# Attention with V read in 8 KB rows: quads of heads and 64x64 tiles for PV

## The chip, the core and the metric

One core of a Trainium2 chip runs the kernel. The metric is the device time of one execution in microseconds (us). The kernel before takes 340.26 us (median of 3 runs, 340.18 to 340.37).

The engines are TensorE (PE, with its weight loads shown apart as PEld), VectorE (DVE), ScalarE (ACT), GpSimd (POOL) and SyncE (SP), which issues the DMA transfers. TensorE reads its operands from SBUF and writes PSUM.

## The reference

```python
B, Hq, Hkv, Sq, Sk, D = 16, 32, 8, 16, 2048, 128     # bfloat16, inputs scaled by 0.05
k = jnp.repeat(k, 4, axis=1)
v = jnp.repeat(v, 4, axis=1)
scores = jnp.einsum("bhqd,bhkd->bhqk", q, k) * D ** -0.5
p = softmax(scores)
return jnp.einsum("bhqk,bhkd->bhqd", p, v)
```

Four query heads share one K/V head, so each of the 128 K/V heads meets 4 x 16 = 64 query rows. K and V are 67.1 MB each, Q and the output 2.1 MB each.

## The kernel before

The unit of work is a pair of K/V heads: 64 units, with 128 query rows (64 per head) by 2,048 keys each.

SP issues all transfers on one queue, in the order of the loop over `t` (L198): K of unit `t` (`load_k`, 1 MB, 128 rows of 8 KB, four buffers `Kn`), Q of four units at a time (`load_q`), the first half of a store, V of a unit further back (`load_v`, 1 MB), the second half of the store. V is read as two rows of 4 KB per partition, one per head; it has eight buffers `Vb`, and `v_lag` puts it two to five units behind K. K waits until the unit four before has been transposed, V until PV of the unit eight before is done, a store until its output is normalised. V of the last unit comes in three pieces (`CUTS`).

Per unit `i`, each engine runs its own list and meets the others at semaphores:

- DVE (`emit`, L350): reads the scores from PSUM, scales and negates them into `Sneg` and takes the row minimum (L353); takes the reciprocal of the row sum before (L361); transposes K of unit `i + 2` in 32x32 blocks, in two instructions (`kt`, L344).
- PE (loop from L282): `scores` of unit `i + 1` (32 matmuls in tiles of 32 rows by 64 columns, 512 columns each: four tiles at a time, one for each row group; every second group of four, L219, uses the weights that L248 loaded); `pv` of unit `i - 3` (L266: 32 matmuls of 128 rows by 64 columns, two column groups); eight transposes of the probabilities (`turn_p`, L257); in two of four units four transposes of Q (`turn_q`, L231), which have a PSUM bank of their own.
- ACT: `exp` into `P` (L391); the norm of unit `i - 3` out of `O_ps` (L409); the copies of the transposed probabilities (`p_out`, L399) and of the transposed Q (`q_out`, L380).
- POOL: spreads Q for the transposes (L152).

PE's loop covers eight units, as do DVE's and ACT's. The scores have one PSUM buffer, so `scores` of a unit waits for L353 of the unit before. The last three units' outputs go to banks of `S_ps`.

## Time and profile before

| | |
|---|---|
| median of 3 runs | 340.26 us |
| profiled execution, own time | 340.08 us |
| its span, first to last instruction | 338.3 us |
| TensorE clock granted, mean | 0.995 |
| bytes moved, mean rate | 138.55 MB, 410 GB/s |
| busy: PE, DVE, ACT, POOL | 278.0, 295.4, 267.8, 31.3 us |
| K, V transfers: issue to landing (median) | 14.9, 15.5 us |

The profile is one execution. Its slices are 40 equal parts of the span, with the busy share in tenths. The DMA row is the mean share of the core's 16 DMA engines. The chain of work is followed back from the last instruction; "SPq" in it is SP's queue of DMA issues. A group's line gives the line of the code, engine, operation and tiles, then busy time, mean ns of one instruction, and the engine's idle time before these instructions with what ended it. Matmuls overlap, so their mean duration is longer than the distance between them.

### The profile page before, as it was taken

What the parts mean: (1) busy time and instruction counts of PE and PEld (TensorE: products, weight loads), DVE (VectorE), ACT (ScalarE), POOL (GpSimd) and SP (SyncE); (2) the same over time, 40 slices, a digit from 0 to 9 for tenths busy, and PEclk for the clock granted to TensorE, in tenths of its full rate; (3) what the DMA queues carried; (4) which work ended last, traced back from release to release, by engine and by line L of the source; (5) the groups of instructions that cost most, each with busy time, mean ns of one, the idle gap of its engine ahead of it and who ended that gap; (6) DMA issues with size and microseconds to landing.
All of it is one profiled execution on the core that took longest, in us unless ns stands there. A gap on an engine that the chain in (4) does not pass through costs nothing.

```text
span 338.3 us, 9752 instructions
## 1 busy us (share of the span) xinstructions
PE 278.0 (82%) x4736; PEld 159.2 (47%) x3712; DVE 295.4 (87%) x321; ACT 267.8 (79%) x355; POOL 31.3 (9%) x22
## 2 busy tenths in 40 slices
PE   0687999979898798979898797787888878888885
PEld 0133555535554454545355454454454454453454
DVE  2499999989998999989999988989889889899860
ACT  1178888888989788978888787877977878778785
POOL 3202020201102020200202010020200202000000
PEclk9979999999999999999999999999999999999999
DMA  7999999999999999999999999999999999999996
GB/s 299 417 417 412 412 412 413 420 416 422 416 417 417 424 414 419 419 417 421 418 421 414 422 418 415 419 419 418 421 417 418 421 414 418 421 418 422 416 413 213
DMA packets 39642, 138.55 MB, mean 410 GB/s; under 512 B 12496, under 2 KB 15056, under 8 KB 31440
## 3 DMA queue, kind: packets, MB, share of 16 engines
q1 hardware_dynamic: 39632, 138.43, 100.7%
q8 instruction: 5, 0.08, 0.1%
q14 instruction: 5, 0.04, 0.0%
HBM read 136.31 MB, written 2.10 MB: 409 GB/s over the span
## 4 chain that ended last, share of the span: by engine, by line
SPq 65%; DMA 18%; DVE 6%; PE 4%; issue 3%; ACT 2%; POOL 1%; ACTq 0%
SPq L195 37%; SPq L163 13%; SPq L171 11%; DMA Kn<-in_k_dram 9%; DMA Vb<-in_v_dram 8%; SPq L184 4%; DVE KT L344 3%; DVE Sneg L353 3%; ACT P L391 2%; DMA Qn<-in_q_dram 1%; PE ST_ps L257 1%; PE S_ps L248 1%; PE ST_ps L231 1%; PE S_ps L219 1%; POOL Q L152 1%
## 5 line engine op out<-in xcount | busy, mean ns | idle before, releaser
L344 DVE STREAM_TRANSPOSE KT<-Kn 128x1024 f32<-128x1024 f32 x128 | 151.5, 1222 | 27.6 <-DMA Kn<-in_k_dram 27.6
L391 ACT ACTIVATE P<-Sneg,nbias 128x2048 bf16<-128x2048 f32 (+1 forms) x65 | 160.1, 2463 | 8.8 <-DVE Sneg L353 8.8
L353 DVE TENSOR_SCALAR_CACHE_REDUCE Sneg<-S_ps 128x2048 f32<-128x2048 f32 x64 | 144.3, 2255 | 6.3 <-PE S_ps L219 6.3
L248 PE MATMUL S_ps<-KT,QT 32*64 32x512 bf16 x1024 | 102.8, 393 | 16.8 <-DVE Sneg L353 15.8
L219 PE MATMUL S_ps<-KT,QT 32*64 32x512 bf16 x1024 | 101.2, 387 | 0.0
L266 PEld LDWEIGHTS O_ps<-Vb,PT 128*64 128x64 bf16 x1952 | 57.2, 110 | 66.4 <-issue 66.4
L266 PE MATMUL O_ps<-Vb,PT 128*64 128x128 bf16 x1952 | 66.2, 220 | 25.7 <-DMA Vb<-in_v_dram 25.7
L399 ACT ACTIVATE PT<-ST_ps 128x512 f32<-128x512 f32 x128 | 69.7, 595 | 19.0 <-PE ST_ps L257 18.4
L257 PE MATMUL ST_ps<-ident,P 128*128 128x128 f32 x512 | 71.0, 282 | 5.9 <-ACT P L391 5.7
L248 PEld LDWEIGHTS S_ps<-KT,QT 32*64 32x64 bf16 x1024 | 28.9, 104 | 84.2 <-issue 47.6
L257 PEld LDWEIGHTS ST_ps<-ident,P 128*128 128x128 f32 x512 | 55.4, 142 | 15.4 <-ACT P L391 11.1
L152 POOL COPY Q<-Qn 128x2048 bf16<-128x2048 bf16 x16 | 30.3, 1893 | 254.2 <-DMA Qn<-in_q_dram 185.2
L409 ACT ACTIVATE O<-O_ps,rrec 128x128 bf16<-128x128 f32 x61 | 22.4, 368 | 30.2 <-PE O_ps L266 29.9
L231 PE MATMUL ST_ps<-ident,Q 128*128 128x128 f32 x128 | 20.4, 284 | 8.6 <-POOL Q L152 7.9
L380 ACT ACTIVATE QT<-ST_ps 128x512 f32<-128x512 f32 x32 | 19.3, 605 | 8.3 <-PE ST_ps L231 8.3
L231 PEld LDWEIGHTS ST_ps<-ident,Q 128*128 128x128 f32 x128 | 15.7, 147 | 9.0 <-issue 7.9
L391 ACT ACTIVATION_READ_ACCUMULATOR P<-Sneg,nbias 128x1 f32 x65 | 13.3, 205 | 0.0
L361 DVE RECIPROCAL rrec<-rowsum 128x1 f32<-128x1 f32 x63 | 9.9, 157 | 0.0
L353 DVE DVE_READ_ACCUMULATOR Sneg<-S_ps 128x1 f32 x64 | 5.3, 82 | 0.0
L266 PE MATMUL S_ps<-Vb,PT 128*64 128x128 bf16 x96 | 3.6, 221 | 0.8 <-DMA Vb<-in_v_dram 0.7
L266 PEld LDWEIGHTS S_ps<-Vb,PT 128*64 128x64 bf16 x96 | 2.9, 110 | 1.6 <-DMA Vb<-in_v_dram 1.1
L372 DVE TENSOR_TENSOR rowsum<-rowsum 128x1 f32<-128x1 f32 x1 | 0.2, 160 | 3.4 <-ACT P L391 3.4
(9 smaller groups left out, 3.7 us busy)
## 6 DMA issues: line engine op xcount, KB each, us to landing
Kn<-in_k_dram SPq DMA_DIRECT2D x64, 1024.0 KB, 14.9
Vb<-in_v_dram SPq DMA_DIRECT2D x63, 1024.0 KB, 15.5
Qn<-in_q_dram SPq DMA_DIRECT2D x16, 128.0 KB, 14.7
out_dram<-O SPq DMA_DIRECT2D x118, 16.0 KB, 14.2
Vb<-in_v_dram SPq DMA_DIRECT2D x1, 512.0 KB, 9.6
Vb<-in_v_dram SPq DMA_DIRECT2D x1, 320.0 KB, 9.8
Vb<-in_v_dram SPq DMA_DIRECT2D x1, 192.0 KB, 9.8
out_dram<-O SPq DMA_DIRECT2D x5, 32.0 KB, 1.9
```

The costliest lines, as they stand in the source:

```text
L163: sp.dma_start(Kn[s][:, :], kf[p]).then_inc(sem_k[p % BODY], 16)
L171: sp.dma_start(dst, vf[:, 2 * p:2 * p + 2, :]).then_inc(sem_v[s], 16)
L195: sp.dma_start(of[128 * p + 64 * x:128 * p + 64 * x + n, :], Osb[s][64 * x:64 * x + n, :]).then_inc(sem_o[s], 16)
L219: return pe.add_instruction(mybir.InstMatmult(name=nc.get_next_instruction_name(), engine=mybir.EngineType.PE, ins=[pe.lower_ap(rhs), pe.l ...
L231: ins = pe.transpose(dst[:, 128 * j:128 * (j + 1)], src[:, j, b, :], ident4[:, :])
L248: ins = pe.matmul(s_ap, w, x, start=(acc == 0), stop=(acc == 3))
L257: ins = pe.transpose(dst[:, 128 * t:128 * (t + 1)], P[p % 2][:, 128 * x:128 * (x + 1)], ident4[:, :])
L266: ins = pe.matmul(o_ap(at)[64 * g:64 * (g + 1), :], pt[:, j // 2, j % 2, 64 * g:64 * (g + 1)], Vb[p % NV][:, g, j, :], start=(j == 0), sto ...
L344: ins = dve.transpose(KT[p % NKT][:, :].rearrange("p (t b e a x) -> p x e t b a", t=J // 2, b=2, e=2, x=2)[:, x, :, :, :, :], Kn[p % NK][: ...
L353: dve.tensor_scalar(Sneg[i % 2][:, :].rearrange("p (t h x) -> p h t x", t=8, h=2), S_ps[:, :].rearrange("p (h t x) -> p h t x", t=8, h=2), ...
L391: act.activation(P[i % 2][:, :].bitcast(BF16)[:, cols].rearrange("p (n y e) -> p n y e", y=64, e=2), Sneg[i % 2][:, cols].rearrange("p (n ...
L399: ins = act.activation(PT[i % NPT][:, 4 * h:4 * (h + 1), :].rearrange("p t q -> p (t q)"), stage_ap(h), ACT.Copy,)
```

## The change

Two units now make a quad of four neighbouring K/V heads `4d` to `4d + 3`.

- K: unit `u = 2d + i` holds heads `4d + i` and `4d + 2 + i`. Partition `2a + g` gets 8 KB of head `4d + 2g + i`, so a transfer reads 128 rows of 8 KB from two places 1 MB apart. There are eight K buffers in one tensor `Kd`.
- V: a transfer is two neighbouring heads, 128 rows of 8 KB, one per partition: 64 partitions per head, 32 groups of 64 keys. There are two buffers `Vd` of a quad (2 MB) each, so V of a quad waits for PV of two quads before (`sem_pv`). V of the last two quads goes into K's buffers 0 to 3. The last two transfers are one of 2 MB in four pieces (rows of 4 KB, 2 KB, 1.25 KB and 0.75 KB).
- The lag of V behind K is 2 and 6 units for the first four, then 11, less one every eight units, down to 7. Stores of the first 28 quads stay in the loop; the last four are issued behind all loads, the very last half by ACT.
- Scores: 32 matmuls in eight tiles (four row groups by two column groups) in turn, each with its own weight load.
- `P` holds a quad, with its two units interleaved, so `turn_p` of a unit needs `exp` of both and comes two units later (`TLAG`). PV is 64 matmuls per unit, 64 rows by 64 columns: two row groups (heads `i`) by two column groups (`g`), in two banks of `O_ps`. It comes six units after the unit's `exp`, half a quad per step.
- `turn_q` is eight transposes of 64 rows for each two units; its output shares the first bank of `ST_ps` with `turn_p`, so `turn_p` of even steps waits for ACT's copy of Q, and `turn_q` waits for ACT's copies of the probabilities (`sem_po`).
- PE's loop covers four units, with the last two quads under an `If` in the same loop. A step of PE is, in this order: scores of the next unit, on even steps `turn_q`, half a quad of PV, on even steps the wait for ACT's copy of Q, `turn_p`. An even step of ACT is `exp`, the copy of Q, two copies of `turn_p`; an odd one `exp`, two copies, two norms.
- DVE transposes K in one instruction per unit instead of two. It takes over the norms of the last four quads, with ACT doing half of the last one.

```diff
-NK = 4
-NV = 8
-NKT = 2
+NK = 8
+NV = 2
+NP = 2
 NPT = 4
-NO = 8
-NQ = 2
+NO = 4
+NQ = 4
 QPAIRS = 4
-BODY = 8
-VLAG = 5
-PVLAG = 3
-SLAG = 10
-QLEAD = 4
-CUTS = (0, 8, 13, 16)
+ROUND = 8
+STEP = 4
+VLAG = 7
+PVLAG = 6
+TLAG = 2
+SLAG = 6
+QLEAD = 6
+CUTS = (0, 16, 24, 29, 32)
...
-    Kn = [sb(f"Kn{i}", [128, 2 * J * 128], BF16) for i in range(NK)]
-    Vb = [sb(f"Vb{i}", [128, 2, J, 128], BF16) for i in range(NV)]
-    KT = [sb(f"KT{i}", [128, 2 * J * 64], F32) for i in range(NKT)]
+    ident = sb("ident", [128, 128], F32)
+    Kd = sb("Kd", [128, NK, 32 * D], BF16)
+    Vd = [sb(f"Vd{i}", [128, 2, J, D], BF16) for i in range(NV)]
+    KT = [sb(f"KT{i}", [128, J * 64], F32) for i in range(2)]
...
-    P = [sb(f"P{i}", [128, Sk // 2], F32) for i in range(2)]
-    PT = [sb(f"PT{i}", [128, J // 2, 128], F32) for i in range(NPT)]
+    P = [sb(f"P{i}", [128, J // 2 * 128], F32) for i in range(NP)]
+    PT = [sb(f"PT{i}", [128, J // 4, 128], F32) for i in range(NPT)]
...
-    ST_ps = ctx.enter_context(nc.psum_tensor("ST_ps", [128, 3 * 512], F32))
-    O_ps = ctx.enter_context(nc.psum_tensor("O_ps", [128, 512], F32))
+    ST_ps = ctx.enter_context(nc.psum_tensor("ST_ps", [128, 2 * 512], F32))
+    O_ps = ctx.enter_context(nc.psum_tensor("O_ps", [128, 2 * 512], F32))
...
-    of = out.rearrange("b h s d -> (b h s) d")
-    kf = k.rearrange("b h s d -> (b h s d)").rearrange("(n a x) -> n a x", n=NP, a=128)
-    vf = v.rearrange("b h s d -> (b h) (s d)").rearrange("g (a x) -> a g x", a=128)
+    of = out.rearrange("b h s d -> (b h s) d").rearrange("(n g i x) d -> n i g x d", n=ND, g=2, i=2)
+    kf = k.rearrange("b h s d -> (b h s d)").rearrange("(n g i a x) -> n i a g x", n=ND, g=2, i=2, a=64)
+    vf = v.rearrange("b h s d -> (b h s d)").rearrange("(n a x) -> n a x", n=NU, a=128)
...
     def v_lag(p):
-        return min(2 + max(p - 4, 0) // 8, VLAG)
+        return 2 if p < 2 else 6 if p < 4 else max(VLAG, 11 - (p - 4) // 8)
+
...
+    def q_ap():
+        return ST_ps[:, 0:512].rearrange("p (b x) -> p b x", b=2)
+
+    def o_ap(d, i):
+        x = 512 * i
+        if d >= ND - 2:
+            return S_ps[:, 1024 * (d % 2) + x:1024 * (d % 2) + x + D]
+        return O_ps[:, x:x + D]
+
+    def v_ap(d, g):
+        if d >= ND - 2:
+            return Kd[:, 2 * (d % 2) + g, :].rearrange("p (j d) -> p j d", j=J)
+        return Vd[d % NV][:, g, :, :]
...
+    def store_both(eng, d, g):
+        dst = of[d, :, g].rearrange("i x d -> x i d")
+        eng.dma_start(dst, Osb[d % NO][64 * g:64 * (g + 1), :, :]).then_inc(sem_o[d % NO], 16)
...
-            def load_k(p):
-                s = p % NK
-                if p >= NK:
-                    sp.wait_ge(sem_kt[(p - NK) % BODY], (p - NK) // BODY + 1)
-                sp.dma_start(Kn[s][:, :], kf[p]).then_inc(sem_k[p % BODY], 16)
+            def load_k(m):
+                s = m % NK
+                if m >= NK:
+                    sp.wait_ge(sem_kt[s], m // NK)
+                sp.add_instruction(mybir.InstDMACopy(
+                    name=nc.get_next_instruction_name(), engine=mybir.EngineType.SP,
+                    ins=sp.lower_ap_dma(kf[m // 2, m % 2]), outs=sp.lower_ap_dma(Kd[:, s, :].unsqueeze(1)),
+                    queue="qSPDynamicHW", mode="Copy", cce_op=ALU.bypass,
+                )).then_inc(sem_k[s], 16)
 
             def load_v(p):
...
+                d, g = divmod(p, 2)
+                if p >= NU - 2:
+                    if g:
+                        return
+                    sp.wait_ge(sem_kt[3], ROUNDS)
+                    for x, (lo, hi) in enumerate(zip(CUTS, CUTS[1:])):
+                        src = vf[p:p + 2, :, D * lo:D * hi].rearrange("g a x -> a g x")
+                        sp.dma_start(Kd[:, 2:4, D * lo:D * hi], src).then_inc(sem_vl[1 + x], 16)
                     return
...
+                if d == ND - 2:
+                    sp.wait_ge(sem_kt[g], ROUNDS)
+                elif d >= NV and g == 0:
+                    sp.wait_ge(sem_pv[d % NV], d // NV)
+                sp.dma_start(v_ap(d, g).rearrange("a j d -> a (j d)"), vf[p]).then_inc(
+                    sem_v[d % NV] if d < ND - 2 else sem_vl[0], 16)
...
+            def turn_q(x):
+                rows = slice(64 * x, 64 * (x + 1))
                 src = Q4[:, :, :, :, :].bitcast(F32).rearrange("p j b r c -> p j b (r c)")
...
+                for b in range(2):
+                    for j in range(QPAIRS):
+                        ins = pe.transpose(q_ap()[:, b, 64 * j:64 * (j + 1)], src[rows, j, b, :], ident[rows, rows])
+                ins.then_inc(sem_qt[x], 1)
+
+            def scores(u):
+                d, i = divmod(u, 2)
+                kt = KT[i][:, :].bitcast(BF16).rearrange("p (b y g e) -> p b e g y", b=2, g=2, e=2)
+                qt = QT[d % 2][:, :, :].bitcast(BF16).rearrange("p b (n e) -> p b e n", e=2)
                 for acc in range(4):
                     b, e = divmod(acc, 2)
...
+                    for z in range(8):
+                        r, g = z % 4, (z + z // 4) % 2
+                        rows = slice(32 * r, 32 * (r + 1))
+                        at = 128 * g + 64 * i
                         ins = pe.matmul(
...
+                            S_ps[64 * g:64 * (g + 1), 512 * r:512 * (r + 1)],
+                            qt[rows, b, e, at:at + 64], kt[rows, b, e, g],
+                            start=(acc == 0), stop=(acc == 3),
                         )
...
+                ins.then_inc(sem_s[u % STEP], 1)
...
+                        y = 8 * (w % 2) + 4 * h + t
+                        ins = pe.transpose(ST_ps[:, 512 * h + 128 * t:512 * h + 128 * (t + 1)],
+                                           P[w // 2 % NP][:, 128 * y:128 * (y + 1)], ident[:, :])
+                    ins.then_inc(sem_pt[h][w % STEP], 1)
...
+            def pv(d, js, gs=(0, 1)):
+                for j in js:
+                    pt = PT[(2 * d + j // 16) % NPT][:, :, :].bitcast(BF16).rearrange("p t (q e) -> p t e q", e=2)
+                    for g in gs:
+                        for i in range(2):
+                            rows = slice(64 * i, 64 * (i + 1))
+                            ins = pe.matmul(
+                                o_ap(d, i)[64 * g:64 * (g + 1), :],
+                                pt[rows, j % 16 // 2, j % 2, 64 * g:64 * (g + 1)],
+                                v_ap(d, g)[rows, j, :],
+                                start=(j == 0), stop=(j == J - 1),
+                                skip_group_check=True,
+                            )
+                return ins
...
+                def step_s(i):
+                    pe.wait_ge(sem_max[i], now)
+                    scores(i + 1)
+
+                def step_q(i):
+                    x = i // 2
+                    if x == 0:
+                        pe.wait_ge(sem_q4, then)
+                    pe.wait_ge(sem_po[(i - TLAG - 1) % STEP], now)
+                    turn_q(x)
+
+                def step_pv(i):
+                    d, half = divmod((i - PVLAG) % STEP, 2)
+                    if half == 0:
+                        pe.wait_ge(sem_v[d], v_now)
+                        pe.wait_ge(sem_nm[1 - d], it)
+                        pe.nop(nofuse=True)
+                    ins = pv(d, range(16 * half, 16 * half + 16))
+                    if half:
+                        ins.then_inc(sem_pv[d], 1)
+
+                def step_pt(i):
+                    w = (i - TLAG) % STEP
+                    if w == 0:
+                        pe.wait_ge(sem_exp[1], now)
+                    pe.wait_ge(sem_po[(w - 1) % STEP], it if w == STEP - 1 else now)
+                    turn_p(w)
+
+                with pe.If(it >= TURNS + 1):
+                    pe.wait_ge(sem_po[1], TURNS + 1)
+                    turn_p(NU - 2)
+                    pe.wait_ge(sem_po[2], TURNS)
+                    turn_p(NU - 1)
+                    pe.wait_ge(sem_vl[0], 32)
+                    pe.nop(nofuse=True)
+                    pv(ND - 2, range(J)).then_inc(sem_pe, 1)
+                    for x, (lo, hi) in enumerate(zip(CUTS, CUTS[1:])):
+                        if lo == 16:
+                            pe.wait_ge(sem_po[3], TURNS + 1)
+                        pe.wait_ge(sem_vl[1 + x], 16)
+                        pe.nop(nofuse=True)
+                        ins = pv(ND - 1, range(lo, hi))
+                    ins.then_inc(sem_pe, 1)
...
+            def kt(u, n):
+                dve.wait_ge(sem_k[u % NK], n)
+                dve.transpose(
+                    KT[u % 2][:, :].rearrange("p (b j a) -> p j b a", b=2, j=J),
+                    Kd[:, u % NK, :].bitcast(F32).rearrange("p (j b c) -> p j b c", b=2, c=32),
+                ).then_inc(sem_kt[u % NK], 1)
...
+                    exp(i, None, sem_exp[i % STEP])
+                    if i % 2 == 0 and not (at.end and i >= 4):
+                        y = (i + 4) // 2
+                        q_out(y % 2, at.num(2, y // 2 + 1))
+                    if at.first or i >= TLAG:
+                        p_out(i - TLAG, at.tile(i - TLAG))
+                    if i % 2 and (at.first or i >= PVLAG + 1):
+                        y = (i - PVLAG - 1) // 2
+                        act.wait_ge(sem_pv[y % NV], at.num(2, y // NV + 1))
+                        if at.first >= 2 or (at.first == 1 and y >= 0):
+                            act.wait_ge(sem_o[y % NO], at.num(64, 64 * (y // NO)))
+                        for z in range(2):
+                            x = (2 * y + z) % ROUND
+                            ins = act.activation(Osb[y % NO][:, z, :], o_ap(y % NO, z), ACT.Copy, scale=rrec[:, x:x + 1])
+                        ins.then_inc(sem_nm[y % NV], 1)
...
```

## The prediction

> **What bounds the kernel now.** I read the page's slices and DMA parts first, then the chain, then a table by stretch, and only then the engines' groups.
>
> ```profile
> DMA  7999999999999999999999999999999999999996
> ...
> DMA packets 39642, 138.55 MB, mean 410 GB/s; under 512 B 12496, under 2 KB 15056, under 8 KB 31440
> ...
> q1 hardware_dynamic: 39632, 138.43, 100.7%
> ...
> SPq 65%; DMA 18%; DVE 6%; PE 4%; issue 3%; ACT 2%; POOL 1%; ACTq 0%
> ```
>
> The DMA engines are full from the second slice to the last but one, and the chain runs mostly through SP's DMA issues (SPq) and the transfers themselves. No compute engine carries more than 6% of it. By stretch (length; PE, PEld, DVE, ACT, POOL busy; clock, DMA share, GB/s):
>
> ```profile
> 0.00:10.00 10.00, 1.36 (x6) 0.99 (x7) 3.38 (x3) 1.88 (x2) 2.85 (x7) 1.00 0.80 319
> ...
> 100.00:200.00 100.00, 85.81 (x1493) 49.47 (x1168) 93.69 (x102) 84.27 (x113) 9.47 (x5) 1.00 1.03 418
> 200.00:300.00 100.00, 82.11 (x1423) 47.94 (x1117) 89.22 (x99) 80.07 (x108) 9.47 (x5) 1.00 1.03 419
> ...
> 330.00:338.00 8.00, 4.81 (x104) 3.70 (x104) 0.33 (x2) 4.58 (x10) 0.00 (x0) 1.00 0.62 216
> ```
>
> A share of 1.03 says that one engine's packets overlap a little and that no gap is left. 10 us at 319 GB/s is 7.6 us of work at 419, so the start loses 2.4 us; the last V piece lands at 335.5 (waits of the last PV) and norm and store take the remaining 2.8. Compute follows the stream, but not by far:
>
> ```profile
> L344 DVE STREAM_TRANSPOSE KT<-Kn 128x1024 f32<-128x1024 f32 x128 | 151.5, 1222 | 27.6 <-DMA Kn<-in_k_dram 27.6
> L391 ACT ACTIVATE P<-Sneg,nbias 128x2048 bf16<-128x2048 f32 (+1 forms) x65 | 160.1, 2463 | 8.8 <-DVE Sneg L353 8.8
> L353 DVE TENSOR_SCALAR_CACHE_REDUCE Sneg<-S_ps 128x2048 f32<-128x2048 f32 x64 | 144.3, 2255 | 6.3 <-PE S_ps L219 6.3
> ...
> L266 PE MATMUL O_ps<-Vb,PT 128*64 128x128 bf16 x1952 | 66.2, 220 | 25.7 <-DMA Vb<-in_v_dram 25.7
> ```
>
> DVE's and PE's longest waits are for DMA. Where nothing waits, Sneg starts come 4.53 us apart (38.43, 42.96, 47.50), with 5.3 per unit over the run. The rates of single pieces, from the timeline:
>
> ```profile
> 308.24 1.09 PE L257 MATMUL ST_ps<-ident,P 128*128 128x128 f32 x8
> ...
> 308.93 1.08 ACT L399 ACTIVATE PT<-ST_ps 128x512 f32<-128x512 f32 x2 [0.22 <-PE ST_ps L257]
> ...
> 309.26 0.42 PE L248 MATMUL S_ps<-KT,QT 32*64 32x512 bf16 x4
> ...
> 309.51 0.39 PE L219 MATMUL S_ps<-KT,QT 32*64 32x512 bf16 x4
> ...
> 309.74 0.39 PE L248 MATMUL S_ps<-KT,QT 32*64 32x512 bf16 x4
> ...
> 312.28 1.09 PE L266 MATMUL O_ps<-Vb,PT 128*64 128x128 bf16 x32 [1.03 <-DMA Vb<-in_v_dram]
> ```
>
> Four score matmuls of 0.39 us, one per row group, fill 0.39 to 0.42: they start within 0.03, and the next four 0.225 us later. Sixteen PV pairs take (1.09 - 0.22)/15 = 58 ns a pair, so two column tiles run side by side.
>
> **The change, step by step.** Base: the profiled execution, 340.08 us (span 338.3 and 1.8 around it); the median is 0.18 more.
>
> *V rows.* The trace's packet records (size, start, duration) give means of 311.0 ns for 8,192 B (K) and 160.0 ns for 4,096 B (V). On one engine the next packet starts 3.2 and 3.7 ns before the end, so the pitches are 307.8 and 156.4 ns. (39,632 packets over 16 engines with 3.5 ns each are 2.6% of the span: the 1.03.) 62 of the 64 V transfers become 128 rows of 8 KB: 496 rows per engine, each in place of two. 496 x (312.8 - 307.8) = 2.5 us less. Ends: 0, if bytes and not packets set the stream's rate; 4.5, if whole durations count (496 x 9.1 ns). I take 2.5, since the pitch is what adds up to the span. The last 2 MB keep rows of 4 KB and less, and stores (256 B rows) and Q loads move the same rows on the same queue: 0.
>
> *K from two places.* Rows stay 8 KB, but neighbouring partitions now come from heads 1 MB apart. Nearest row: V before, two heads 512 KB apart, ran at the 160 ns above. So 0; ends: no gain is open, as rows were 8 KB; if they cost as two 4 KB rows, 512 x 5.0 ns = 2.6 us more.
>
> *SP's order and its new wait.* SP issues K, stores, V; V of a quad waits for PV of two quads earlier, and Q, K and stores stand behind it. Ahead of the first such wait are 16 K, 4 V, 6 Q: 21.8 MB, at 419 GB/s 51.9 us, done at 54.3 with the start. PV of quad 0 ends in step 7: Sneg 6 starts at 43.0, +2.3, exp 2.7 and some 0.6 of ACT lag (four steps of 4.7 against 4.53, below) gives 48.5, Q copy 0.6, eight P transposes 1.1, scores 1.0, PV half 0.9: 52.2. The first bytes move 1.7 us after the first issue (0.7 to 2.4): 53.9, before 54.3. So 0, with 0.4 to spare; ends 0 and 2 us (slow tiles, next). Later the stream holds five transfers (12.5 us) between a quad's last V and the next waiting V, PV takes a step and a half-step (6.2): 4.6 to spare, and the store's wait for the norm stands one wait behind, on work already done. POOL's Q copy (1.9) waits for the second Q transposes and has two steps, 9.4, until the next: 0.
>
> *Scores.* Eight tiles in turn instead of four, with a weight load each (32, were 16): four rounds of 0.225 = 0.9 us, was 1.8; ends 0.9 and 1.8. *PV.* 64 matmuls per unit with 64 rows; row groups overlap in the scores and column groups in PV, so four at once: 16 x 58 ns = 0.93 us; ends 0.93 and 1.86. No row has both kinds at once. Both lie beside DVE and ACT; what counts is the chain.
>
> *The shared staging bank.* Q transposes now use P's first bank, so on even steps: exp 2.58 (with its accumulator read, as rows stand), Q copy 0.6, then P transposes may start, 0.05 + 0.69 to the first copy (308.24 to 308.93), copies 1.08: 5.0. Odd steps: 2.58 + 1.08 + two norms 0.7 = 4.4. ACT needs 9.4 per two units, 4.7 each. DVE has one transpose in place of two (2.3 to 2.4) and stays at 4.5. The stream asks for less: K 0 lands near 5, the last K eight V before the end (333 - 20 = 313), 308/63 = 4.88 per unit. ACT's 4.7 hides under that with 0.18 a unit; if that cover goes, each 0.1 costs up to 6 us over 61 steps, less what the early K and the V waits absorb (some 5 us).
>
> *The end.* After the last K: transpose 2.4, Sneg 2.3 twice, exp in halves 3, both units' copies, done 16 us on; PV of quad 30 1.9, of 31 mostly before its last piece: 19 against the stream's 20. So the last piece ends it as now: 12 matmuls, norm, store, 2.8. Ends 0 and 2.7 (PV at half rate: two quads and the last pieces). DVE's and ACT's norms and ACT's own store run side by side: 0.
>
> Sum: 340.08 - 2.5 = 337.6, median **337.8 us**; own range 336.0 to 339.6.
>
> **Rivals.**
>
> *A. PV doesn't run at four tiles (slower).* At 29 ns per matmul (58/2) PV takes 1.86 per unit. In the odd step PE ends the even step's P transposes 4.35 after exp's start, then scores 1.05, PV 1.86 and 0.69 to the first copy: 7.95, later than exp's end at 7.6; with copies 1.08 and norms 0.7 the cycle is 9.75 (4.88 a unit, all cover gone), about 1 us of stream is lost near the first V wait, and the end is 2.7 late: 337.8 + 3.7 = 341.5. Taken as linear from 14.5 ns (0) to 29 (3.7), it eats the 2.5 from 24 ns per matmul on. For it: PV's own row shows nothing faster. Against: four score matmuls start within 30 ns. [...]
>
> *B. Neither tile form overlaps.* Scores stay 1.8 too: 4.35 + 1.95 + 1.86 + 0.69 + 1.78 = 10.6, 5.3 a unit: (5.3 - 4.88) x 61 = 26 us, 363. Against it: both overlaps stand in the rows, apart.
>
> *C. K's new layout slows its packets* (engines meeting at the same partitions). K's packets are 512 x 308 ns = 158 us per engine; 5% more is 8 us, 346. No row for or against the destination side.
>
> *D. Bytes set the rate:* 340.2, no change; the even 411 to 424 GB/s of the slices speak for it, the packet records against.
>
> *E. Whole durations count:* 340.26 - 4.5 = 335.8.
>
> **Chances.** Forecast 0.60, A 0.13, B 0.05, C 0.06, D 0.09, E 0.07. Within 0.2% (0.7 us) is no change here: D and a slice of A, 0.10; slower: the rest of A, B, C, 0.22; faster 0.68. Range 335.4 to 342.5: it takes in E and A and leaves B and most of C out.
>
> **What would show it.** Fewer packets (about 31,700), DMA share still 1.02 in the middle at some 422 GB/s, chain on SPq again; eight score matmuls in one group of 0.4; PV spans near 0.93 per 64 matmuls; ACT waiting for PE after Q copies by 0.7. Wrong would be: slices with DMA below 9 near 54 us or later, K packets longer than 311 ns, PE or ACT leading the chain, a tail over 3 us after the last V piece.

## The result and the profile after

The changed kernel takes 353.02 us (median of 4 runs, 352.80 to 353.29) beside 340.31 us of the kernel before on the same chip: a ratio of 1.037, 95% interval 1.036 to 1.039. It is slower by 12.7 us; 2.5 us less were forecast. The profiled execution took 353.29 us with a span of 351.5.

The page of the changed kernel, its slices, its DMA parts and the first line of the chain:

```profile
PEclk9956869999999999999999999999999989999998
...
DMA  7999993699999999999999999999999999999993
GB/s 275 426 415 419 414 402 137 267 397 419 423 418 394 418 422 425 418 420 424 421 423 420 422 426 420 421 421 422 423 419 422 421 421 423 424 424 419 329 407 110
...
DMA packets 31659, 138.57 MB, mean 394 GB/s; under 512 B 12448, under 2 KB 15008, under 8 KB 15520
...
q8 instruction: 6, 0.10, 0.1%
...
PE 42%; ACT 28%; DMA 10%; issue 10%; DVE 4%; SPq 4%; POOL 1%; ACTq 0%
```

Three things differ from before. There are about 8,000 packets fewer, as meant. The DMA row has a hole in the seventh and eighth slices, and the GB/s row a dip in the last three. The chain no longer runs through SP's issues but through PE, ACT and "issue", time in which an engine waited for nothing that the profile shows. The clock granted to TensorE (PEclk) is low in the third to the sixth slice. By stretch (length; PE, PEld, DVE, ACT, POOL busy; clock, DMA share, GB/s):

```profile
56.00:60.00 4.00, 3.86 (x104) 2.50 (x88) 4.00 (x5) 2.73 (x4) 1.89 (x1) 1.00 0.02 8
60.00:64.00 4.00, 4.00 (x106) 2.23 (x104) 3.85 (x2) 3.59 (x5) 0.00 (x0) 1.00 0.00 0
100.00:200.00 100.00, 90.26 (x2264) 52.51 (x2256) 93.75 (x85) 84.43 (x116) 9.46 (x5) 1.00 1.02 418
200.00:300.00 100.00, 89.77 (x2185) 51.81 (x2169) 92.35 (x81) 82.58 (x112) 9.46 (x5) 0.98 1.02 422
```

From 56.5 to 63 us next to nothing moves. From 200 to 300 us the stream runs at 422 GB/s, which was 419 before; from 100 to 200 us, in which SP stands 4.2 us at a further V wait (to 111.4), it is 418 both before and after. SP's issues around the hole, from the timeline of the changed kernel:

```profile
51.42 0.54 SPq L187 DMA_DIRECT2D Kd<-in_k_dram  x1
63.13 0.33 SPq L207 DMA_DIRECT2D Vd<-in_v_dram  x1
```

SP stands for 11.2 us at the wait of `load_v` for PV of quad 0, whose second half PE does at 61.99 to 63.08. PE is late because its own list stood still in its first turn (the timeline again; idle time before an instruction in brackets):

```profile
19.47 1.56 PE L269 MATMUL S_ps<-KT,QT 32*64 32x512 bf16 x23 [5.30 <-issue]
...
24.97 1.08 PE L269 MATMUL S_ps<-KT,QT 32*64 32x512 bf16 x9 [3.94 <-issue]
...
38.44 1.77 PE L280 MATMUL ST_ps<-ident,P 128*128 128x128 f32 x8 [2.89 <-issue]
```

The scores of one unit stop after 23 of 32 matmuls, with every operand there. (Of the 5.30 us before their first part, 2.4 are the wait for DVE, whose `Sneg` of unit 0 ends at 16.5.) Beside these stops the trace has the six 16 KB packets of the row "q8 instruction": at 16.7, 22.5, 29.1, 35.3, 41.2 and 46.8 us, and none later. Each takes 1.0 to 1.1 us, and the three starts above come 1.5 to 2.1 us after the end of such a packet. Before, there were four in the same stretch, at 21.9, 30.9, 41.6 and 49.3 (and a fifth at 333.5); the page before has

```profile
q8 instruction: 5, 0.08, 0.1%
```

The low clock stands beside the stops: 0.50 was granted from 20 to 26 us and 0.52 from 26 to 32, and the eight P transposes of 1.09 us take 1.77 at 38.44, where 0.56 was granted.

To see where the time is, I counted for each stretch what the stream lost against 421.5 GB/s (length less the bytes of the kernel's own transfers over that rate), up to the landing of the last V, and the rest of the span as the end:

| us | 0 to 10 | 10 to 48 | 48 to 80 | 80 to 305 | 305 to last load | end | span |
|---|---|---|---|---|---|---|---|
| before | 2.6 | 0.8 | 0.4 | 1.6 | 1.4 | 3.3 | 338.3 |
| after | 3.1 | 0.5 | 10.1 | 0.7 | 2.7 | 6.2 | 351.5 |
| difference | +0.6 | -0.2 | +9.7 | -0.9 | +1.2 | +3.0 | +13.2 |

So the questions were: why PV of quad 0 is late (9.7 us), and what the end is made of (3.0 us).

### The profile page after: what moved, and what is told of

The parts are those of the page before. It is cut to its first block, busy times and chain, and to the rows that moved or that the text cites. A ratio compares the mean times of both kernels' runs of the same rounds, so it can differ in the third digit from the quotient of the medians.

```text
span 351.5 us, 15443 instructions
## 1 busy us (share of the span) xinstructions
PE 284.7 (81%) x6912; PEld 166.0 (47%) x6912; DVE 293.5 (83%) x264; ACT 260.8 (74%) x348; POOL 31.3 (9%) x22
## 4 chain that ended last, share of the span: by engine, by line
PE 42%; ACT 28%; DMA 10%; issue 10%; DVE 4%; SPq 4%; POOL 1%; ACTq 0%
PE S_ps L269 19%; ACT P L454 15%; PE ST_ps L280 13%; PE O_ps L290 9%; DMA Vd<-in_v_dram 7%; ACT PT L463 5%; DVE Sneg L403 4%; ACT QT L445 4%; ACT O L493 3%; DMA Kd<-in_v_dram 2%; SPq L222 2%; DMA Qn<-in_q_dram 1%; PE ST_ps L256 1%; SPq L207 1%; DVE KT L395 1%
## 5 line engine op out<-in xcount | busy, mean ns | idle before, releaser
L395 DVE STREAM_TRANSPOSE KT<-Kd 128x2048 f32<-128x2048 f32 x64 | 147.0, 2297 | 12.9 <-DMA Kd<-in_k_dram 12.7
L269 PE MATMUL S_ps<-KT,QT 32*64 32x512 bf16 x2048 | 128.4, 624 | 26.8 <-DVE Sneg L403 16.8
L280 PE MATMUL ST_ps<-ident,P 128*128 128x128 f32 x512 | 71.9, 285 | 20.1 <-ACT QT L445 13.2
L290 PEld LDWEIGHTS O_ps<-Vd,PT 64*64 64x64 bf16 x3840 | 56.3, 108 | 33.3 <-issue 31.7
L280 PEld LDWEIGHTS ST_ps<-ident,P 128*128 128x128 f32 x512 | 56.7, 144 | 29.3 <-issue 25.6
L290 PE MATMUL O_ps<-Vd,PT 64*64 64x128 bf16 x3840 | 65.8, 219 | 4.4 <-DMA Vd<-in_v_dram 4.3
L256 PEld LDWEIGHTS ST_ps<-ident,Q 64*128 64x128 f32 x256 | 19.7, 148 | 35.8 <-issue 34.9
L256 PE MATMUL ST_ps<-ident,Q 64*128 64x64 f32 x256 | 24.3, 240 | 9.3 <-POOL Q L176 8.6
L493 ACT ACTIVATE O<-O_ps,rrec 128x128 bf16<-128x128 f32 x56 | 17.6, 375 | 0.0
L290 PE MATMUL S_ps<-Kd,PT 64*64 64x128 bf16 x256 | 4.6, 218 | 1.0 <-DMA Kd<-in_v_dram 0.7
L290 PEld LDWEIGHTS S_ps<-Kd,PT 64*64 64x64 bf16 x256 | 3.9, 107 | 1.7 <-issue 1.7
```

The lines of the kernel that those rows point to most:

```text
L256: ins = pe.transpose(q_ap()[:, b, 64 * j:64 * (j + 1)], src[rows, j, b, :], ident[rows, rows])
L269: ins = pe.matmul(S_ps[64 * g:64 * (g + 1), 512 * r:512 * (r + 1)], qt[rows, b, e, at:at + 64], kt[rows, b, e, g], start=(acc == 0), stop= ...
L280: ins = pe.transpose(ST_ps[:, 512 * h + 128 * t:512 * h + 128 * (t + 1)], P[w // 2 % NP][:, 128 * y:128 * (y + 1)], ident[:, :])
L290: ins = pe.matmul(o_ap(d, i)[64 * g:64 * (g + 1), :], pt[rows, j % 16 // 2, j % 2, 64 * g:64 * (g + 1)], v_ap(d, g)[rows, j, :], start=(j ...
L395: dve.transpose(KT[u % 2][:, :].rearrange("p (b j a) -> p j b a", b=2, j=J), Kd[:, u % NK, :].bitcast(F32).rearrange("p (j b c) -> p j b c ...
L493: ins = act.activation(Osb[y % NO][:, z, :], o_ap(y % NO, z), ACT.Copy, scale=rrec[:, x:x + 1])
```

## The experiments

The columns "48 to 80", "late" (305 us to the last load) and "end" are counted as above, on each run's profiled execution. Ratios are to the kernel before, measured on the same chip beside them.

| run | median us (lowest to highest) | ratio, 95% interval | 48 to 80 | late | end |
|---|---|---|---|---|---|
| x1_tail_after | 346.80 (346.35 to 346.86) | 1.017 to 1.020 | 2.5 | 2.2 | 8.2 |
| x3_dead | 352.31 (351.89 to 352.61) | 1.034 to 1.037 | 9.7 | 2.0 | 6.1 |
| x4_sp_store | 350.14 (349.75 to 351.13) | 1.028 to 1.031 | 8.9 | 2.3 | 4.6 |
| y1_v8k | 337.18 (337.08 to 338.39) | 0.991 to 0.994 | 0.2 | 1.2 | 3.3 |
| x6_dead34 | 347.14 (346.68 to 347.67) | 1.019 to 1.022 | 2.2 | 2.4 | 8.2 |
| z1_end_sp | 349.53 (348.64 to 350.49) | 1.026 to 1.030 | 6.6 | 2.7 | 4.6 |
| z2_after_sp | 345.65 (344.36 to 346.44) | 1.013 to 1.018 | 2.5 | 3.4 | 5.6 |
| y2_kpair | 340.81 (340.43 to 341.08) | 1.0005 to 1.0023 | 0.4 | 1.4 | 3.2 |
| x7_dead34 | 354.57 (353.80 to 354.93) | 1.039 to 1.043 | 9.3 | 2.7 | 8.6 |
| y4_dead_before | 340.26 (340.18 to 341.00) | 0.999 to 1.001 | 0.5 | 1.5 | 3.2 |
| z3_v60 | 347.50 (346.96 to 348.49) | 1.019 to 1.024 | 1.7 | 1.3 | 10.9 |
| x5_stride | 350.88 (350.26 to 351.50) | 1.028 to 1.034 | 7.3 | 3.1 | 6.2 |
| z4_stride | 343.94 (343.46 to 345.82) | 1.009 to 1.013 | 0.1 | 1.5 | 6.3 |
| z5_stride4 | 344.46 (343.58 to 344.56) | 1.011 to 1.014 | 0.7 | 3.6 | 5.9 |

### TensorE's last block behind the loop

PE's loop body begins with a block for the last two quads (`If(it >= TURNS + 1)`, L346), which 17 of its 18 turns jump over. Here it stands behind the loop.

```diff
-            with pe.Fori(0, TURNS + 2) as it:
+            with pe.Fori(0, TURNS + 1) as it:
...
-                with pe.If(it >= TURNS + 1):
-                    pe.wait_ge(sem_po[1], TURNS + 1)
-                    turn_p(NU - 2)
...
+            pe.wait_ge(sem_po[1], TURNS + 1)
+            turn_p(NU - 2)
...
```

> TensorE's block for the last two quads (about 540 instructions, 34 KB at 64 B each) stands behind the loop instead of at the head of its body, where it was jumped over in 17 of 19 turns. The same work is done. Theory (code): the first turn waits because everything in the body, jumped over or not, is first fetched in 16 KB pieces, about 6 us apart while the DMA queue is full; six such pieces lie between 16.6 and 46.8 us of the changed kernel. With 34 KB less ahead of the first turn two of them go: the first eight Sneg follow each other at 5 us or less, PV of quad 0 ends some 6 to 11 us earlier than 63, the gap in the DMA near 56 to 64 us shrinks from 9 to 3 us or less, and the time falls from 353.0 to 343 to 347 us, unless the code now has to be fetched at the end, up to +6 us there. Rival (lag): the V waits are simply one step too early for the chain of scores, exp, transposes and PV at its own pace; then the gap and the 353 us stay within 1 us.

346.80 us: 6.2 less. PE's scores of unit 1 run through; the timeline of this run:

```profile
16.37 2.01 PE L269 MATMUL S_ps<-KT,QT 32*64 32x512 bf16 x32 [2.43 <-DVE Sneg L402]
```

In place of "issue" it waited for DVE, as it should. `Sneg` of unit 1 starts at 18.46 us (26.09 in the changed kernel), P transposes of unit 0 at 29.7 (38.4), PV of quad 0 ends at 54.0 (63.1), V of quad 2 is issued at 54.08, and the hole shrinks to a dip (this run's windows):

```profile
52.00:56.00 4.00, 3.61 (x112) 2.12 (x104) 3.85 (x5) 3.60 (x6) 0.00 (x0) 1.00 0.86 331
56.00:60.00 4.00, 3.39 (x107) 1.99 (x92) 4.00 (x5) 3.21 (x5) 0.00 (x0) 1.00 0.99 418
```

The first turn now has four 16 KB packets in place of six. Two of them for the block's 544 matmuls, transposes and weight loads make 60 bytes an instruction, an estimate from these two counts, good to within one packet of the two; the expectation had 64. But the block has to be fetched at the end: a packet comes at 336.4 us, and within the last quad's PV PE stands for 2.4 us on "issue":

```profile
335.95 0.55 PE L290 MATMUL S_ps<-Kd,PT 64*64 64x128 bf16 x25 [0.23 <-issue]
338.91 0.78 PE L290 MATMUL S_ps<-Kd,PT 64*64 64x128 bf16 x39 [2.41 <-issue]
```

So 7.6 us were won in the early hole, and 2 lost at the end.

### Dead code at the loop's head: two attempts that asked nothing

```diff
+                with pe.If(it >= TURNS + 3):
+                    pv(ND - 2, range(J))
```

> The changed kernel with a block at the head of TensorE's loop body that no turn executes (128 matmuls, and their weight loads, 16 KB of instructions). The same work is done. Theory (code): one more 16 KB piece has to be fetched in the first turn, PV of quad 0 ends 4 to 7 us later, the DMA gap near 56 us grows as much, 353.0 becomes 357 to 360 us. Rival (lag): an If that is never taken costs 0.1 us a turn at most; 353 to 355 us and the same gap.

> The run with TensorE's last block behind the loop (346.8 us), with a block of the same length, 34 KB of instructions that no turn executes, put at the loop's head in its place. The same work is done. A dead block of 16 KB on top of the 34 KB changed nothing (352.3), so the bytes jumped over do not count. Theory (jump): what costs is that the first turn jumps to code that had not been fetched ahead; then the block at the head alone brings the loss back, whatever stands in it: scores of unit 1 stall by 4 to 5 us after 20 or so matmuls, P transposes of unit 0 start near 38 us instead of 29.7, the DMA gap near 56 us is 8 us again, 352 to 354 us. Rival (the move helped in another way, by the loop's extra turn or its waits): 346 to 348 us, and no stall in unit 1.

The first was made on the changed kernel, the second (34 KB of such code, two PV of a quad and two `turn_p`) on the version above. 352.31 and 347.14 us, no stall added. The expectation of the second took the first as evidence against the bytes; both were void. The condition cannot hold for the loop's range, and the programs that ran hold a branch and no block. They serve as repeats: 353.02 and 352.31, 346.80 and 347.14, with the same six and four instruction packets in the first turn.

### Dead code that is really there

```diff
+                with pe.If(pe.snap(it * 3) == 4):
+                    pv(0, range(J))
+                    pv(0, range(J))
+                    turn_p(NU - 2)
+                    turn_p(NU - 1)
```

> The run with TensorE's last block behind the loop, with 34 KB of instructions at the loop's head that no turn executes, this time behind a condition on the loop's counter that the builder cannot decide ahead: in the two dead-block runs before, the listing shows a plain branch and no block, so they asked nothing. The same work is done. Theory (code): the first turn jumps past what was fetched ahead; scores of unit 1 stall by 4 to 5 us after some 23 matmuls, P transposes of unit 0 start near 38 us instead of 29.7, the DMA gap near 56 us is 8 us again, and 347 becomes 352 to 355 us. Rival (moving the block helped by another way than the code's place): 346 to 348 us and no stall in unit 1.

354.57 us: all of the loss is back, by code that is never executed and stands where the block stood. The hole is there again, beside the stop for the last block at the end (8.6 us). One line of the windows and two of the timeline of this run:

```profile
56.00:60.00 4.00, 3.86 (x104) 2.66 (x104) 4.00 (x5) 2.73 (x6) 1.89 (x1) 1.00 0.03 12
...
18.88 1.99 PE L269 MATMUL S_ps<-KT,QT 32*64 32x512 bf16 x25 [4.80 <-issue]
24.11 0.65 PE L269 MATMUL S_ps<-KT,QT 32*64 32x512 bf16 x7 [3.25 <-issue]
```

There are six instruction packets in the first turn again, two more than without the block, at 16.1, 21.8, 28.3, 34.2, 39.9 and 45.5 us. The cause is the place of the code in the loop, not what it computes: six packets and 9.3 us lost from 48 to 80 us with this block, six and 10.1 with the one that is executed once, four and 2.5 with neither at the loop's head. That PE's stops are waits for code is read from the packets of 16,384 bytes beside them in the first turn (in the changed kernel three starts come 1.5 to 2.1 us after the end of one). There no such packet comes between 46.8 us and the end, although each turn jumps back over what took up to six of them. Whether the two additional packets are the block itself, brought in though it is jumped over, or belong to the jump's target, these runs do not tell.

### The block at the end of the loop body, and the last store by SP

The block stands behind `step_pt(3)`, still in the loop, and SP issues both last stores.

> The changed kernel with TensorE's last block at the end of the loop body instead of its head, and the last half store issued by SP. The same work is done. By the jump theory the start is as with the block behind the loop (gap near 56 us 1 us or less), and the 2.4 us that TensorE waited for code within the last quad's PV (336.5 to 338.9 in that run, beside a 16 KB instruction packet at 336.4) go if the block was fetched with the loop before: 353.0 - 6.2 - 2.9 - 2.4 = 341.5 us. If the block is fetched only when it is first entered, 344 to 346 us.

349.53 us: neither of the two expected values, and a spread of 1.9 us among the four runs (348.64 to 350.49). The end has no stop for code any more (4.6 us), but the first turn has its stop in another place, where it jumps over the block on its way back to the loop's head: the first scores of the second turn start late. The timeline of this run:

```profile
42.97 2.02 PE L269 MATMUL S_ps<-KT,QT 32*64 32x512 bf16 x32 [6.15 <-issue]
```

A hole of 6.6 us in the stream follows. In the loop the block costs at the start (6.15 us of "issue" here), behind it at the end (2.41 in x1_tail_after).

### The same dead code in the kernel before

The condition is the one of x7_dead34, with eight `pv(0, 0)` behind it.

> The kernel before with 32 KB of instructions at the head of TensorE's loop that no turn executes. The same work is done. Theory (two causes are needed, the late code and V waits without slack): scores of unit 1 stall here too, by 4 to 9 us, but this kernel's transfers wait for nothing that is as close, so the DMA stays full for longer and 340.3 becomes 340 to 344 us. Rival (late code alone costs its delay): 346 us or more.

340.26 us, no change (0.999 to 1.001), with six instruction packets in place of four; two of them for the block's 512 matmuls and weight loads make 64 bytes an instruction, an estimate as coarse as the one above. `Sneg` of units 1 and 2 starts 1.9 and 4.0 us later than in the kernel before (21.97 for 20.11, 28.72 for 24.68), that of unit 6 still 3.9 us later (46.89 for 42.96), and the stream does not notice. The windows of this run, and below them those of the kernel before:

```profile
48.00:56.00 8.00, 7.67 (x128) 4.16 (x98) 8.00 (x11) 7.05 (x10) 1.89 (x1) 1.00 1.02 413
56.00:64.00 8.00, 7.53 (x136) 4.48 (x106) 8.00 (x11) 7.14 (x12) 0.00 (x0) 1.00 1.02 411
```

```profile
48.00:56.00 8.00, 7.25 (x129) 3.85 (x92) 8.00 (x10) 7.02 (x11) 0.00 (x0) 1.00 1.04 420
56.00:64.00 8.00, 7.74 (x136) 5.08 (x112) 7.50 (x9) 7.13 (x12) 0.00 (x0) 1.00 1.02 409
```

So code that comes late is not enough. It costs where a DMA wait with no slack follows PE, and that wait is the change's: V of quad 2 stands behind PV of quad 0 in SP's one queue. Two limits remain: the delay here is 3.9 us and not 9, and no run gives the changed kernel more slack at this wait, so that both are needed is read from the pair of kernels.

### The last store by SP

```diff
-                for g in range(2) if d < ND - 1 else [0]:
+                for g in range(2):
                     store_both(sp, d, g)
...
-            act.wait_ge(sem_nm[(ND - 1) % NV], normed(ND - 1))
-            act.wait_ge(sem_end, 1)
-            store_both(act, ND - 1, 1)
```

> The changed kernel with the last half store issued by SP, behind the other, instead of by ACT. The same work is done. In the changed kernel ACT's issue takes 2.62 us (347.03 to 349.65), and the span ends 5.3 us after the last norm began, against 2.8 from last landing to end before. Theory (ACT's first own transfer is slow): the end shrinks by 2 to 3 us, 350 to 351 us. Rival (the end is long because of the norms on two engines or of the pieces of V): 352.5 to 353.5 us.

350.14 us. Of the 2.9 us less the end has 1.6 (6.2 to 4.6); the rest lies in the early hole (10.1 to 8.9), where the first packet of code came 1.1 us earlier. x3_dead, with the same code and ACT's store, has its first packet early too (15.8 us) and a hole of 9.7, so this part is put down to chance and not to the store. The end after the last norm, changed kernel and this run:

```profile
346.28 0.37 ACT L505 ACTIVATE O<-S_ps,rrec 128x128 bf16<-128x128 f32 x1 [4.87 <-issue]
347.03 2.62 ACTq L162 DMA_DIRECT2D out_dram<-O  x1
```

```profile
344.76 0.37 ACT L505 ACTIVATE O<-S_ps,rrec 128x128 bf16<-128x128 f32 x1 [5.27 <-issue]
345.22 1.25 SPq L162 DMA_DIRECT2D out_dram<-O  x2
```

ACT's one issue takes 2.62 us, SP's two 1.25; from the end of the issue to the end of the span it is 1.9 us both times (349.65 to 351.5, 346.47 to 348.3). Beside the issue an 8 KB instruction packet stands at 347.7 us, so ACT too may wait for code there; but one stands at 346.4 us in this run as well, where ACT issues nothing, and what makes the issue slow stays open. The remaining 1.3 us over the kernel before fits SP's 1.25 for two stores of 32 KB, one behind the other, after the last norm: before, the last store was issued behind one norm on ACT, and the span ended 1.95 us after it. No run tries this part apart.

Together with the block behind the loop:

> The changed kernel with both: TensorE's last block behind the loop, and the last half store issued by SP. The same work is done. The two losses lie in different places (the first 64 us, the last 6), so they should add: 353.0 - 6.2 - 2.9 = 343.9 us, 343.4 to 344.4. If the later landing of the last V had hidden part of the store's cost, 345 to 346.

345.65 us, in the band named for a hidden store, but the store is not hidden: it is worth 1.2 us here between medians whose runs spread over 2.1 us. The end shrinks by 2.6 (8.2 to 5.6), the late loss grows by 1.2 (2.2 to 3.4), and the expectation had taken over all of the 2.9, of which only 1.6 were the end's.

### Rows of 8 KB, and K from two places, each alone

Both were made on the kernel before.

```diff
-                    dst = Vb[s][:, :, :, :].rearrange("a g j d -> a g (j d)")
-                    sp.dma_start(dst, vf[:, 2 * p:2 * p + 2, :]).then_inc(sem_v[s], 16)
+                    dst = Vb[s][:, :, :, :].rearrange("a g j d -> a (g j d)")
+                    sp.dma_start(dst, vw[p]).then_inc(sem_v[s], 16)
```

> The kernel before with V read as one 8 KB row per partition in place of two 4 KB rows, and nothing else changed: V's rows land in other places than PV takes them from, so the output is another one, with the same amount of work. Theory (pitch of packets): 512 x 5.0 ns per engine less, 340.3 becomes 337.7 us, 31,400 or so packets. Rival (bytes set the rate): 340.3 us. Rival (whole durations count): 335.7 us.

337.18 us, 3.0 less (ratio 0.991 to 0.994). That is the forecast's term (2.5 to 2.6), and neither 0 nor 4.5; packets of 8,192 bytes take 310.6 ns on average, as before (310.8). So the gain is real, and stands alone in a kernel whose waits have slack.

```diff
-                sp.dma_start(Kn[s][:, :], kf[p]).then_inc(sem_k[p % BODY], 16)
+                sp.add_instruction(mybir.InstDMACopy(
+                    name=nc.get_next_instruction_name(), engine=mybir.EngineType.SP,
+                    ins=sp.lower_ap_dma(kw[p // 2, p % 2]), outs=sp.lower_ap_dma(Kn[s][:, :].unsqueeze(1)),
+                    queue="qSPDynamicHW", mode="Copy", cce_op=ALU.bypass,
+                )).then_inc(sem_k[p % BODY], 16)
```

> The kernel before with K read as the changed kernel reads it, neighbouring partitions from two heads 1 MB apart, by its form of transfer; the rows land in other places than the scores take them from, so the output is another one, with the same amount of work. Theory (rows of 8 KB cost the same wherever they lie): K packets 311 ns, 340.2 us. In the changed kernel 8 KB packets took 314 ns; if the layout makes them longer by those 3 ns, 512 x 3 ns = 1.5 us more, 341.7. Rival C of the prediction: 5% longer packets, 346 to 348 us.

340.81 us, 0.5 more (0.2 to 0.8 by the interval); the packets take 311.8 ns for 310.8. K's layout costs about half a microsecond, and rival C is out. In the changed kernel itself 8 KB packets average 313.9 ns over the whole run, but 309.7 from 120 to 300 us, where the kernel before has 309.6: the longer ones lie outside the steady part.

### How far apart the scores' operands lie

After the code and the store the version z2_after_sp is still 8.5 us above rows of 8 KB alone. Its stream loses 2.5 us at the first V waits and 3.4 late, so its compute may be late too. Scores of a unit take 1.99 us where 0.9 were forecast.

```diff
-                kt = KT[i][:, :].bitcast(BF16).rearrange("p (b y g e) -> p b e g y", b=2, g=2, e=2)
+                kt = KT[i][:, :].bitcast(BF16).rearrange("p (b g e y) -> p b e g y", b=2, g=2, e=2)
```

> The changed kernel with the scores' moving operand read from neighbouring elements instead of every fourth one (it pairs other values, so the output is another one). Scores of a unit take 1.99 us, eight tiles in 0.45, where the prediction had 0.9. Theory (reading two bytes of every eight from SBUF is what limits eight streams): 0.9 to 1.1 us per unit. Rival (no more than four of these tiles run at a time, wherever they read): 1.99 us again. The time itself follows the chain: with 1 us less per unit the wait for PV of quad 0 ends 4 us earlier, 347 to 350 us; else 353.

350.88 us (two runs), between the two times that were expected; the scores take 1.07 us per unit once the clock is granted in full. The groups, changed kernel and this run:

```profile
L269 PE MATMUL S_ps<-KT,QT 32*64 32x512 bf16 x2048 | 128.4, 624 | 26.8 <-DVE Sneg L403 16.8 <-issue 9.2 <-ACT QT L445 0.7
```

```profile
L269 PE MATMUL S_ps<-KT,QT 32*64 32x512 bf16 x2048 | 78.0, 421 | 35.3 <-DVE Sneg L403 25.8 <-issue 8.8 <-ACT QT L445 0.7
```

Eight tiles do run at once; reading every fourth element (two bytes of every eight) is what holds them to the pace of four (1.99 us a unit; the kernel before, with four tiles at a time, takes as long: 304.60 to 306.59 us). The clock says the same: with every fourth element a unit's scores take 2.02 us where 0.50 is granted (28.45 us in the changed kernel) and 1.99 where 1.00 is (32.92), while with neighbours they take 1.93 at 49.69 us of this run, with 0.66 granted from 48 to 52 us (0.79 over 48 to 56, 0.92 over 52 to 56), and 1.07 at 58.53 us, with 1.00 from 56 to 60. The next two runs are z2_after_sp with neighbours, and with every second element (`p (b g y e)`):

> The changed kernel with TensorE's last block behind the loop, the last half store by SP, and the scores' moving operand read from neighbouring elements instead of every fourth (it pairs other values, so the output is another one). Still open: code and store account for 7 of the 13 us, and 345.6 us is left against 337.2 for 8 KB rows alone. Theory (compute is late: scores of 1.99 us instead of 1.07 in a chain that the V waits follow): scores go to 1.07, PV of quad 0 ends 2 to 4 us earlier, before the stream runs dry; the losses of 1.5 us near 64 to 72 and 2.0 us in 312 to 336 go, and 345.6 becomes 341 to 343 us, the rest being TensorE's wait for code in the last quad (2.1) and the rest of the end. Rival (the waits would be late with any scores): 345 to 346.

> As the run beside it, with the scores' moving operand at every second element, the spacing of the kernel before, where a score matmul took 0.39 us (it pairs other values, so the output is another one). Every fourth element gave 1.99 us per unit, neighbours 1.07. Theory (the spread of bytes read sets the eight tiles' pace): 1.07 to 1.5 us per unit, and a time between 341 and 345.6. Rival (any spacing costs the same): 1.99, 345 to 346.

343.94 and 344.46 us, with 1.07 and 1.11 us for a unit's scores. The loss at the first V waits goes from 2.5 to 0.1 and 0.7, as the theory said; the window of z5_stride4 (every second element) has no dip left:

```profile
52.00:56.00 4.00, 2.67 (x96) 2.06 (x96) 4.00 (x5) 4.00 (x7) 0.00 (x0) 1.00 1.00 397
56.00:60.00 4.00, 3.15 (x104) 2.47 (x88) 4.00 (x5) 2.82 (x4) 0.00 (x0) 1.00 1.02 428
```

The time falls by 1.2 to 1.7 us only, not by 3 to 5. PE's 2.15 us for code in the last quad stay in both, and the late loss stays with every second element (3.6). With neighbours it goes to 1.5, but the profiled execution is the slowest of its five (345.82) and loses 4.3 us in 80 to 305 us, with slower work on PE (P transposes of 307 ns on average for 285 in the changed kernel, PV matmuls of 226 for 219) and slices in which the clock granted is 0.7 to 0.8. So the operands' distance explains the losses at the first V waits and about a sixth of the 8.5 us in time; what else keeps the later V waits and the end long stays open, but for the 2.15 us of code.

### V of the next-to-last quad ahead of a wait

```diff
+    for p in (60, 61):
+        v_behind[p + VLAG].remove(p)
+        v_behind[57 + VLAG].append(p)
```

In the changed kernel SP stands from 319.4 to 326.3 us at V of unit 58, which waits for PV of quad 27, and V of units 60 and 61 is queued behind it.

> The changed kernel with TensorE's last block behind the loop, the last half store by SP, and V of units 60 and 61 (which goes into K's buffers and waits for no PV) issued ahead of V of unit 58 (which waits for PV of quad 27). The same work is done. Theory: between 312 and 336 us the stream loses 2.0 us in the run without this because SP stands at that wait while two transfers that need no wait are queued behind it; with them ahead the loss goes to 0.5 or less, 345.6 becomes 343.5 to 344.5. Rival (the end is set by compute, PV of quad 29 now being later): 345.5 or more.

347.50 us, 1.9 more than without it. The late loss did go from 3.4 to 1.3, and the last load lands 3.2 us earlier (334.5), but the end grows to 10.9: PV of quad 29 now waits for its V, and all behind it on PE moves.

```profile
329.59 3.63 PE L293 MATMUL O_ps<-Vd,PT 64*64 64x128 bf16 x128 [4.68 <-DMA Vd<-in_v_dram]
...
341.01 0.78 PE L293 MATMUL S_ps<-Kd,PT 64*64 64x128 bf16 x39 [1.06 <-issue]
```

The rival was right: the end of the changed kernel is as much PE's as the stream's. No version tried with the new tiles beats the kernel before.

## Why the prediction was wrong

- **SP's order and its new wait** is the step that failed. Its DMA side came out: with the block behind the loop the engines begin to idle at 54.4 us, 54.3 were forecast. (In the changed kernel the last packets end at 56.0 to 56.5, since the last K ahead of the wait is itself issued late, at 51.42 us for 42.70.) Its PE side put the end of PV of quad 0 at 52.2; it was 63.1. The step took `Sneg` of unit 6 from the trace of before (43.0); it started at 52.9 in the changed kernel. With the block behind the loop it starts at 43.9, and PV ends at 54.0. So 9.1 us of the 10.9 come with the late code, a cause that the ledger did not have. 7.6 of them are there at `Sneg` of unit 1 (26.09 for 18.46); the rest builds up at later stops and under a lower clock (0.62 granted from 44 to 50 us, 1.00 with the block behind the loop), and these two were not taken apart. The block at the head of PE's loop was in the diff, and the row "q8 instruction" stood on the page of before; that kernel's first turn has four packets too, and their delays do not reach its stream.
- The other 1.8 us of the same step ate the margin of 0.4: from `Sneg` of unit 6 to the end of PV it is 10.2 us and not 9.2, and 0.9 come before it. With the block behind the loop this stretch loses 2.5 us, a little over the step's own upper end of 2 us, and largely for the reason that was named, slow tiles: with faster scores the loss is 0.1 and 0.7 (z4_stride, z5_stride4).
- **Scores:** 1.99 us came out, above the upper end of 1.8. The step took the overlap of eight tiles from rows in which the operand had every second element, and did not notice that the new layout makes it every fourth.
- **PV** was right: 64 matmuls in 1.09 us, four at a time, where 0.93 and a start were forecast; rival A is out. (1.09 - 0.22) / 63 is 14 ns per matmul, where rival A had 29.
- **V rows** was right: 422 GB/s from 200 to 300 us, and 3.0 us alone for a forecast of 2.5. Rivals D and E fall with it. **K from two places** was right within 0.5 us.
- **The end** was taken as 0, and ACT's own store "side by side" as free. It is 3.0 us: 1.6 for ACT's issue (x4_sp_store), and by the reading above 1.3 for stores one behind the other. The named upper end of 2.7 was there for PV, not for stores.
- **The shared staging bank** keeps the forecast order, but its waits are longer. ACT waits 1.18 us for the P transposes behind a copy of Q (303.01 us in the changed kernel) where 0.74 was forecast, and 0.41 on odd steps (306.98) where none was. Its cycle came out at 4.82 us per unit for the forecast 4.7 (`Sneg` starts repeat 5.06, 4.51, 5.20, 4.51), which leaves 0.06 to the 4.88 of the stream. The group of the copies before and after:

```profile
L399 ACT ACTIVATE PT<-ST_ps 128x512 f32<-128x512 f32 x128 | 69.7, 595 | 19.0 <-PE ST_ps L257 18.4
...
L463 ACT ACTIVATE PT<-ST_ps 128x512 f32<-128x512 f32 x128 | 69.8, 595 | 55.8 <-PE ST_ps L280 55.8
```

- The sum: -2.5 was about right for the rows alone (3.0 in y1_v8k; 1.1 us of it can be seen in the changed kernel's stretches without holes), and above it lie 9.7 for the hole, 3.0 for the end, 1.2 for the late V waits and 0.6 at the start. The slower rivals asked for slow tiles or slow packets, and none of them was an engine whose code comes late. The list of signs had the hole in it ("slices with DMA below 9 near 54 us or later"), but no step had its cause.

## What to carry to other kernels

When a change puts a transfer behind an engine's work, make the ledger from the first turn of that engine in the new program, its code included: a block that is rarely executed belongs out of the way of the first turns, and the margin has to hold the delay of such code (7.6 us at unit 1 here). A kernel with slack can hide such delays, as the one before did (`Sneg` of unit 6 3.9 us late, 340.26 us all the same), so its time says nothing of their price. A tile layout should be costed with the distance between the elements it reads (1.07 us for neighbours, 1.99 for every fourth), and the last store by its own issue (2.62 us on ACT here).

## What the runs showed of the hardware that was not expected

- Where PE stands for code in its first turn, a 16 KB packet comes every 5.7 to 6.5 us (16.1 to 45.5 us in x7_dead34) while the DMA engines are full, though the packet itself takes 1.0 to 1.1 us. The runs with and without two such packets more differ by 7.8 us (x1_tail_after 346.80, x7_dead34 354.57).
- Code that is never executed opened nearly the same hole as the block that is executed once (9.3 us in x7_dead34, 10.1 in the changed kernel), and it cost nothing in the kernel before (340.26).
- A unit's 32 score matmuls in eight tiles take 1.07 us with neighbouring elements, 1.11 with every second and 1.99 with every fourth; the last hardly changes with the granted clock (2.02 at 0.50), the first nearly doubles (1.93 where 48 to 52 us of x5_stride had 0.66).
- ACT's first transfer of its own takes 2.45 to 2.62 us to issue at the end (x3_dead, the changed kernel), SP's about 0.6.
